# Attention over eight heads per operation, a feed-forward over 512-token blocks with another smelu, and interleaved issue

## The chip, the cores and the metric

One Trainium2 chip, one of its cores. A core has five engines with queues of their own: PE (TensorE, matmuls), DVE (VectorE), ACT (ScalarE), POOL (GpSimd) and SP (which here only issues DMAs). The metric is device time in microseconds (us) of one execution. A *ratio* is the mean time of one kernel's fast runs over the mean of the other's in the same rounds on the same chip, so it is not quite the ratio of the medians that are quoted.

## The reference, cut to what matters

```python
batch, n_heads, seq, head_dim = (4, 8, 768, 48)
for t in range(S):                                    # linear attention with a decaying state
    cur = np.einsum('bhd,bhe->bhde', u[None] * kt, vt)
    y[:, :, t] = np.einsum('bhd,bhde->bhe', rt, state + cur)
    state = w[None, :, :, None] * state + np.einsum('bhd,bhe->bhde', kt, vt)
# y becomes x: 3072 tokens x 384
h = x @ w_in                                          # 384 -> 2048
g = np.where(h >= 1, h, np.where(h <= -1, 0.0, (h + 1) ** 2 / 4))   # smelu
return g @ w_out                                      # 2048 -> 384
```

Both kernels do the attention in chunks of 128 tokens: products of R and K with powers of w, a transposition of both, a masked 128 x 128 matrix AT of their products, AT times V plus the state's share, and a step of the state. The u term is a separate number per token and head, `diag`.

## The kernel before

It goes batch by batch, chunk by chunk and head by head. A feed-forward block of 256 tokens follows each pair of chunks. Cuts are marked with `...`.

```python
for b in range(B):
    ...
    for c in range(NCH):
        for h in range(H):
            ...                                                   # three loads of 24 KB
            nc.gpsimd.tensor_copy(V, Vf)
            nc.vector.tensor_mul(RWp, R, Wpow[h])                 # all 128 x 48
            nc.vector.tensor_mul(KWi, K, Winv[h])
            nc.gpsimd.tensor_mul(KWr, K, Wrev[h])
            nc.gpsimd.tensor_mul(RK, K, u_bc[h])
            nc.vector.tensor_tensor_reduce(scr, R, RK, 1.0, 0.0, ALU.mult, ALU.add, accum_out=diag)
            ...                                                   # 2 transposes, 2 ACT copies of 48 x 128
            nc.tensor.matmul(AT_p, KWiT, RWpT, start=True, stop=True)
            nc.vector.tensor_mul(AT, AT_p, umask)
            ...                                                   # y, state step, output: 3 matmuls, 3 small operations
        if (midx + 1) * 128 % MT == 0:                            # MT = 256
            do_moe_chunk((midx * 128) // MT)

# in do_moe_chunk, for each of the 16 blocks of d_ff:
hT_p = ps.tile([128, MT], F32, name="hT_p", tag="c")              # 2 PSUM buffers, shared with y_p
... # 3 matmuls into hT_p
nc.vector.tensor_scalar(tmp, hT_p, -1.0, 1.0, ALU.max, ALU.min)
nc.scalar.activation(tmp, tmp, AF.Square, bias=half_col, scale=0.5)
nc.scalar.activation(tmp2, hT_p, AF.Relu, bias=neg1_col, scale=1.0)
nc.gpsimd.tensor_add(gT, tmp, tmp2)
... # 2 matmuls of the second layer, which need gT at once
```

## Time and profile before

| | before |
|---|---|
| time, median of 5 | 503.6 us (500.5 to 504.6) |
| span of the profiled run | 501.4 us |
| PE, DVE, ACT, POOL busy | 76, 68, 60, 65% |
| granted PE clock, mean | 0.79 |
| instructions | 10,027 |

The head of the page gives busy us, share of the span and number of instructions by engine; the clock row has the granted PE clock in tenths, in 40 slices of the span:

```profile
...
PE 379.6 (76%) x2184; PEld 180.3 (36%) x2184; DVE 341.4 (68%) x1576; ACT 302.5 (60%) x928; POOL 324.4 (65%) x993
...
PEclk9999999956956967958958859859658659669579
...
```

The groups, costliest first. A line names the source line, engine, operation, output and inputs, shape, count; then busy us in all and mean ns of one; then the engine's idle time just before, with what ended most of it:

```profile
...
L137 PE MATMUL op<-w_out_sb,gT 128*128 128x384 bf16 x384 | 107.1, 365 | 29.4 <-POOL gT L135 25.6
...
L133 ACT ACTIVATE tmp<-tmp,half_col 128x256 f32<-128x256 f32 x192 | 97.4, 507 | 35.5 <-DVE tmp L132 30.3
L132 DVE TENSOR_SCALAR tmp<-hT_p 128x256 f32<-128x256 f32 x192 | 79.7, 420 | 43.0 <-PE hT_p L125 34.3
L180 ACT COPY RWpT<-T_p 48x128 bf16<-48x128 bf16 x192 | 49.6, 258 | 75.3 <-PE T_p L178 68.9
...
L169 POOL TENSOR_TENSOR KWr<-K,Wr 128x48 bf16<-128x48 f32 x192 | 58.5, 305 | 3.3 <-DMA K<-in_k_dram 3.2
...
```

No engine is full. Every operation of the attention is there 192 times, at 209 to 305 ns for 48 or 128 columns. The table of waits (engine, line and tile that waited, what ended it, us in all, times, longest) begins with the handover of the smelu:

```profile
...
PEld L137 <- POOL gT L135: 70.3, 152, 1.1
...
```

The windows view gives busy us of PE, weight load, DVE, ACT and POOL in a stretch, then the granted clock, the DMA share and GB/s. In the middle of the run no engine is above 86%, and PE has three quarters of its clock:

```profile
...
200.00:300.00 100.00, 85.34 (x505) 41.05 (x505) 78.59 (x370) 60.95 (x200) 69.83 (x227) 0.75 0.22 45
...
```

### The profile page before, as it was taken

How to read it: one execution, taken by the hardware profiler on the slowest of the kernel's cores; microseconds unless marked ns; L12 is line 12 of the kernel's file. 1: busy time of each engine (PE TensorE's matmuls, PEld its weight loads, DVE VectorE, ACT ScalarE, POOL GpSimd, SP SyncE). 2: the span in 40 equal slices, each digit the busy share in tenths (PEclk: the TensorE clock that was granted, in tenths of full speed). 3: DMA queues.
4: the chain of work that ended last, by engine and by line, in shares of the span. 5: the costliest groups of instructions: out<-in, count | busy, mean ns of one | idle time of the engine just before them, and what ended most of it. 6: DMA issues, size and time to landing. Idle time of an engine off the chain costs nothing. (4 is left out here: it accounts for less than half of the span.)

```text
span 501.4 us, 10027 instructions
## 1 busy us (share of the span) xinstructions
PE 379.6 (76%) x2184; PEld 180.3 (36%) x2184; DVE 341.4 (68%) x1576; ACT 302.5 (60%) x928; POOL 324.4 (65%) x993
## 2 busy tenths in 40 slices
PE   0004668978778889888879888888799798798874
PEld 0002234433343343344434433434434443443431
DVE  1243666876776877878778778768768768778632
ACT  3996226736736747737747547567457457467465
POOL 5652446846756856857847848758748757768344
PEclk9999999956956967958958859859658659669579
DMA  8942211032032023032122122121231221221100
GB/s 230 238 101 37 40 33 30 25 63 42 10 71 49 13 69 52 10 76 49 39 50 44 43 52 38 48 51 30 57 52 21 54 49 26 54 52 25 38 1 32
DMA packets 89693, 26.24 MB, mean 52 GB/s; under 512 B 83872, under 2 KB 89248, under 8 KB 89248
## 3 DMA queue, kind: packets, MB, share of 16 engines
q1 hardware_dynamic: 88864, 25.20, 22.4%
q0 software_dynamic: 768, 0.40, 1.7%
q14 instruction: 44, 0.36, 0.2%
q8 instruction: 17, 0.28, 0.2%
HBM read 20.84 MB, written 4.72 MB: 51 GB/s over the span
## 5 line engine op out<-in xcount | busy, mean ns | idle before, releaser
L137 PE MATMUL op<-w_out_sb,gT 128*128 128x384 bf16 x384 | 107.1, 365 | 29.4 <-POOL gT L135 25.6
L125 PE MATMUL hT_p<-xTt,w_in_sb 128*128 128x256 bf16 x576 | 116.0, 316 | 5.2 <-ACT tmp_10630 L134 1.3
L133 ACT ACTIVATE tmp<-tmp,half_col 128x256 f32<-128x256 f32 x192 | 97.4, 507 | 35.5 <-DVE tmp L132 30.3
L132 DVE TENSOR_SCALAR tmp<-hT_p 128x256 f32<-128x256 f32 x192 | 79.7, 420 | 43.0 <-PE hT_p L125 34.3
L180 ACT COPY RWpT<-T_p 48x128 bf16<-48x128 bf16 x192 | 49.6, 258 | 75.3 <-PE T_p L178 68.9
L192 POOL CAST state_bf<-state 48x48 bf16<-48x48 f32 x192 | 40.9, 218 | 82.2 <-PE y_p L196 41.8
L178 PE MATMUL T_p<-ident,RWp 128*48 128x128 bf16 x192 | 51.3, 267 | 45.0 <-DVE RWp L165 36.0
L206 DVE SCALAR_TENSOR_TENSOR x_sb<-V,diag,y_p 128x48 bf16<-128x48 bf16 x192 | 50.2, 263 | 45.5 <-PE y_p L196 30.6
L189 DVE TENSOR_TENSOR AT<-AT_p,umask 128x128 bf16<-128x128 f32 x192 | 55.1, 287 | 31.4 <-PE AT_p L187 29.8
L125 PEld LDWEIGHTS <-w_in_sb 128*128 128x128 bf16 x576 | 51.8, 107 | 33.6 <-issue 13.9
L169 POOL TENSOR_TENSOR KWr<-K,Wr 128x48 bf16<-128x48 f32 x192 | 58.5, 305 | 3.3 <-DMA K<-in_k_dram 3.2
L167 DVE TENSOR_TENSOR KWi<-K,Wi 128x48 bf16<-128x48 f32 x192 | 58.6, 305 | 0.0
L175 DVE CUSTOM_DVE_ANT_0 scr<-R,RK 128x48 f32<-128x48 f32 x192 | 54.4, 283 | 6.2 <-POOL RK L172 6.0
L165 DVE TENSOR_TENSOR RWp<-R,Wp 128x48 bf16<-128x48 f32 x192 | 57.1, 297 | 0.1
L187 PE MATMUL AT_p<-RWpT,KWiT 48*128 48x128 bf16 x192 | 49.2, 256 | 8.8 <-ACT KWiT L184 8.1
L172 POOL TENSOR_TENSOR RK<-K,ub 128x48 f32<-128x48 f32 x192 | 54.5, 284 | 0.0
L195 PE MATMUL y_p<-V,AT 128*128 128x48 bf16 x192 | 40.7, 212 | 17.5 <-DVE AT L189 15.5
L137 PEld LDWEIGHTS <-gT 128*128 128x128 bf16 x384 | 26.0, 103 | 74.0 <-POOL gT L135 70.3
L200 DVE SCALAR_TENSOR_TENSOR state<-state,wc,st_p 48x48 f32<-48x48 f32 x192 | 47.6, 248 | 0.6
L162 POOL CAST V<-Vf 128x48 bf16<-128x48 f32 x192 | 43.3, 227 | 0.8 <-issue 0.2
L199 PE MATMUL st_p<-V,KWr 128*48 128x48 bf16 x192 | 42.3, 220 | 0.1
L178 PEld LDWEIGHTS <-RWp 128*48 128x48 bf16 x192 | 21.7, 113 | 51.7 <-DVE RWp L165 38.2
(808 smaller groups left out, 600.4 us busy)
## 6 DMA issues: line engine op xcount, KB each, us to landing
R<-in_r_dram SPq DMA_DIRECT2D x192, 24.0 KB, 1.8
K<-in_k_dram SPq DMA_DIRECT2D x192, 24.0 KB, 1.8
Vf<-in_v_dram SPq DMA_DIRECT2D x192, 24.0 KB, 1.8
out_dram<-o_sb SPq DMA_DIRECT2D x24, 192.0 KB, 2.0
w_in_f<-in_moe_w_in_dram SPq DMA_DIRECT2D x1, 3072.0 KB, 15.6
w_out_f<-in_moe_w_out_dram SPq DMA_DIRECT2D x1, 3072.0 KB, 30.2
w_bc<-in_w_dram POOLq DMA_DIRECT2D x8, 24.0 KB, 8.5
ub<-in_u_dram POOLq DMA_DIRECT2D x8, 24.0 KB, 8.7
```

Of the source, the lines that this page charges most:

```text
L125: nc.tensor.matmul(hT_p, w_in_sb[:, kk, n * 128 : (n + 1) * 128], xTt[:, kk, :], start=(kk == 0), stop=(kk == nKb - 1),)
L132: nc.vector.tensor_scalar(tmp, hT_p, -1.0, 1.0, ALU.max, ALU.min)
L133: nc.scalar.activation(tmp, tmp, AF.Square, bias=half_col, scale=0.5)
L137: nc.tensor.matmul(out_psl[j], gT[:, j * 128 : (j + 1) * 128], w_out_sb[:, n, :], start=(n == 0), stop=(n == nN - 1),)
L165: nc.vector.tensor_mul(RWp, R, Wpow[h])
L167: nc.vector.tensor_mul(KWi, K, Winv[h])
L169: nc.gpsimd.tensor_mul(KWr, K, Wrev[h])
L172: nc.gpsimd.tensor_mul(RK, K, u_bc[h])
L175: nc.vector.tensor_tensor_reduce(scr, R, RK, 1.0, 0.0, ALU.mult, ALU.add, accum_out=diag)
L178: nc.tensor.transpose(T_p[:D, :], RWp, ident)
L189: nc.vector.tensor_mul(AT, AT_p, umask)
L206: nc.vector.scalar_tensor_tensor(out=y_dst, in0=V, scalar=diag, in1=y_p, op0=ALU.mult, op1=ALU.add,)
```

## The change

Its intent: fewer and larger operations, less on the slow paths, and PE always with something to do. It has five parts. (1) Blocks hold one chunk of all four batches, so 512 tokens are one feed-forward tile. (2) Attention operations take all eight heads at once; heads are paired in 128 partitions, 64 for each, so that the two heads' matmuls lie in different rows of the array. (3) smelu is `max(h, square(clip))`, with the clip in a saturating activation. (4) Python generators interleave attention of chunk m+1, first layer of m and second layer of m-1. (5) Setup and loads are fewer and larger. Buffers change with it: three PSUM banks for the first layer, two for the second, three for attention. The diff's core:

```diff
-    ps = ctx.enter_context(tc.tile_pool(name="ps", bufs=2, space=bass.MemoryType.PSUM))
-    ops = ctx.enter_context(tc.tile_pool(name="ops", bufs=1, space=bass.MemoryType.PSUM))
+    ps_h = ctx.enter_context(tc.tile_pool(name="ps_h", bufs=3, space=bass.MemoryType.PSUM))
+    ps_o = ctx.enter_context(tc.tile_pool(name="ps_o", bufs=2, space=bass.MemoryType.PSUM))
+    ps_a = ctx.enter_context(tc.tile_pool(name="ps_a", bufs=3, space=bass.MemoryType.PSUM))
...                                   # attention of one unit: one batch, one chunk, eight heads
+        nc.gpsimd.tensor_mul(Kw[:, :, 0:D], K, Winv)          # K, R, V are 128 x 8 x 48
+        nc.gpsimd.tensor_mul(Rw[:, :, 0:D], R, Wpow)
+        nc.scalar.copy(V, Vf)
+        nc.gpsimd.tensor_mul(KU, K, u3)
+        nc.gpsimd.tensor_mul(KU, KU, R)
+        nc.vector.reduce_sum(diag, KU, axis=mybir.AxisListType.X)
+        yield
...                                   # 8 transposes
+        nc.scalar.copy(RK, tr)                                # 128 x 1024
+        yield
+        for p in range(NP):
+            for s in range(2):
+                rows = slice(s * DP, s * DP + D)
+                mm(AT_p[s][:, p, :], KT[rows, p, :], RT[rows, p, :], start=True, stop=True)
...
+            nc.vector.tensor_mul(a, AT_p[s], umask4)          # twice, 128 x 512
+        yield
...                                   # state and y matmuls, state step
+        nc.gpsimd.tensor_mul(VD, V, diag[:, :, None].to_broadcast([128, H, D]))
+        nc.vector.tensor_add(x.rearrange("q (h d) -> q h d", h=H), VD, y)
...                                   # first layer
-            nc.vector.tensor_scalar(tmp, hT_p, -1.0, 1.0, ALU.max, ALU.min)
-            nc.scalar.activation(tmp, tmp, AF.Square, bias=half_col, scale=0.5)
-            nc.scalar.activation(tmp2, hT_p, AF.Relu, bias=neg1_col, scale=1.0)
-            nc.gpsimd.tensor_add(gT, tmp, tmp2)
+        nc.scalar.activation(cl, h_p, IDENTITY_SAT240, scale=240.0)
+        nc.scalar.activation(sq, cl, AF.Square, bias=0.5, scale=0.5 / 240.0)
+        nc.vector.tensor_max(gT[m][:, n, :], sq, h_p)         # h_p is read last here
...
+    run_all(attention_steps(0))
+    for m in range(NCH + 1):
+        att = attention_steps(m + 1) if m + 1 < NCH else iter(())
+        for n in range(nN):
+            if m < NCH:
+                layer1(m, n)
+            if m > 0:
+                layer2(m - 1, n)
+            want = (n + 1) * 5 * B // nN
+            drain(att, want - done)
```

## The prediction

> **What bounds the kernel now.** No engine is saturated: the page's busy shares are PE 76%, DVE 68%, POOL 65%, ACT 60%. It is bound by many small operations handed round five engines. PE busy is mostly latency: the matmuls stream 411,000 columns, 171 us at full clock, a third of the 501 us span. The groups show 192 attention operations of each kind (24 blocks x 8 heads), each mostly fixed cost: POOL products of 48 columns 284–305 ns, ACT copies 258 ns, DVE 248–305 ns. The feed-forward runs 192 tiles of 256: DVE clip 420, ACT Square 507, ACT Relu 460, POOL add about 730 ns. The waits say the same: the weight load of the second layer waits 70 us for the POOL add. The windows table gives a granted clock of 0.71–0.76 from 100 to 480 us. The start costs 35 us (PE's first matmul): 16 activation-table loads of 1.28 us, DMA issues of w and u interleaved with them, and whole-weight loads ahead of the first inputs.
>
> **What the change does, costed.** DVE clip and Relu disappear; saturating activation and Square (ACT) plus max (DVE) replace them, 96 tiles of 512. From the copies (258 ns at 128 columns, 482 at 384: about 146+0.875/column) cl is 0.6 us and Square about 0.7. DVE from PSUM, 287 ns at 128 and 420 at 256, gives 0.69 us at 512. POOL, 305 ns at 48 and 730 at 256, is 2.04 ns/column, so 0.99 us at 384. The Trainium skill ("GPSIMD Engine Reference", section 3.1) gives 2.6 cycles per element for two inputs, 2.2 ns: agrees. So fixed costs fall eightfold on POOL but the column cost stays.
>
> Estimates per stage of 512 tokens (4 attention units, 16 tiles):
> - ACT: 16 x 1.3 + 4 x 2.05 + 4 x 0.48 = 31 us, 27–28 with the overlap of neighbours seen in the timeline.
> - PE: 49,000 feed-forward columns = 20.6 us warm; 140 small attention matmuls at about 80 ns = 11 us; 32 us.
> - POOL: 4 x (5 x 0.99 + 3 x 0.6) = 27 us.
> - DVE: 16 x 0.69 + 4 x 3.2 = 24 us.
>
> All engines are near balance, PE and ACT first. Fewer instructions: PE 1,480 matmuls from 2,184; POOL about 200 from 993.
>
> **Critical path.** Start: the fourth unit's K, R, V queue behind half a dozen loads, about 6 MB at the 230 GB/s of the early slices, 26–28 us; its chain of about 9 us follows, so the first layer starts near 38 us; only 3 table loads. Then 28 us (first stage, no second layer), four full stages at 35–38 us (PE's 32 plus waits of in-order queues), 24 us without attention, 10 us of second layer alone, 4 us tail: about 250–265.
>
> **Predicted: 258 us, range 230 to 300.** Faster 0.98, same 0.01, slower 0.01.
>
> **What would show it.** Page: PE about 70–75% busy or more with 1,480 matmuls; ACT 65–75%; POOL 60–65% at about 1.0 us per product of 384. Windows: first layer starting at 35–42 us; stages of 33–39 us; granted clock at 0.85 or more, since the array is fed more densely. The skill ("TensorE: Matmul & The Clock Gate", Part 1) says sustained activity releases the clock; before averages 0.79. Waits: no long wait on the smelu chain; attention handoffs (transposes waiting for POOL, AT for ACT's 1,024-column copy) remain.
>
> **What would make it wrong.** A clock that stays at 0.75 makes PE 42 us per stage (about 300). POOL slower on strided or broadcast operands (above 1.3 us) would make it the bound, about 36 us per stage. Three shared attention PSUM buffers and in-order queues could serialise units to over 10 us each. Downward: small matmuls nearer 55 ns and little coupling give 230.

## More of the kernel before

A scheduler in the kernel framework sets the final order of each engine's queue.

## The result, and the profile after

| | before | after |
|---|---|---|
| time, median of 5 | 503.6 us | 242.1 us (240.1 to 242.4) |
| ratio | | 0.480 (95%: 0.478 to 0.482) |
| span of the profiled run | 501.4 us | 238.4 us |
| PE, DVE, ACT, POOL busy | 76, 68, 60, 65% | 77, 58, 69, 62% |
| granted PE clock, mean | 0.79 | 0.97 |
| instructions | 10,027 | 4,187 |

The head of the page after, with the busy tenths of PE and POOL and the clock in 40 slices of 6 us each:

```profile
...
PE 182.6 (77%) x1480; PEld 100.0 (42%) x1480; DVE 137.2 (58%) x245; ACT 164.3 (69%) x296; POOL 148.6 (62%) x197
...
PE   0033543796398296789797999899999999999994
...
POOL 5297857979899998889999897955653000000000
PEclk9999999999859769999999999999999999999999
...
```

PE's share is the same as before, but in half the time. What to see is the shape: POOL at eight or nine tenths from the tenth slice to the 26th but for one, then falling to nothing, and PE full only towards the end. The groups that answer to those of before:

```profile
...
L255 DVE TENSOR_TENSOR gT<-sq,h_p 128x512 bf16<-128x512 f32 x96 | 64.0, 682 | 27.1 <-ACT sq L254 26.7
L254 ACT ACTIVATE sq<-cl 128x512 f32<-128x512 f32 x96 | 59.6, 635 | 1.6
L253 ACT ACTIVATE cl<-h_p 128x512 f32<-128x512 f32 x96 | 56.2, 597 | 13.3 <-PE h_p L250 12.8
...
L165 POOL TENSOR_TENSOR KU<-K,u_bc 128x384 f32<-128x384 f32 x24 | 24.0, 1001 | 2.2 <-DMA K<-in_k_dram 2.2
L226 POOL TENSOR_TENSOR VD<-V,diag 128x384 f32<-128x384 bf16 x24 | 19.9, 830 | 8.4 <-ACT V L163 6.6 <-DVE diag L168 1.5
...
```

Eight heads in one POOL product cost 1.00 us, where eight products of one head took 8 x 0.30 = 2.4 us. The windows by stretch say which engine sets the pace:

```profile
...
43.00:75.00 32.00, 24.58 (x183) 12.79 (x183) 17.82 (x33) 24.11 (x43) 29.52 (x34) 0.89 0.56 111
75.00:106.00 31.00, 21.13 (x173) 11.44 (x171) 17.21 (x34) 19.18 (x37) 28.27 (x37) 0.89 0.29 64
106.00:137.00 31.00, 27.71 (x252) 15.22 (x250) 23.12 (x44) 26.38 (x50) 29.30 (x38) 1.00 0.69 143
137.00:168.00 31.00, 29.72 (x272) 16.10 (x271) 23.66 (x45) 28.46 (x52) 23.31 (x31) 1.00 0.30 70
168.00:200.00 32.00, 31.64 (x276) 17.54 (x276) 21.00 (x36) 29.51 (x54) 9.00 (x12) 1.00 0.09 32
200.00:238.00 38.00, 34.78 (x210) 18.52 (x208) 14.13 (x22) 24.61 (x47) 0.00 (x0) 0.99 0.13 47
...
```

From 43 to 137 us POOL (the fifth busy figure) is at 87.1 of 94 us; from 168 us PE is at 31.6 of 32. That is work and not latency: the matmuls that start from 168 to 200 us stream 71,500 columns, an estimated 30.2 us at 216 ns for 512. ACT, at 29.5 us, is close behind. Three of the longest waits:

```profile
...
DVE diag L168 <- POOL KU L166: 40.1, 11, 12.6
DVE gT L255 <- ACT sq L254: 26.7, 29, 5.0
...
PEld L172 <- POOL KWi_158 L160: 13.0, 2, 11.6
...
```

The first is the one that matters. DVE executes its queue strictly in order. In that queue stands the sum `diag` of a later unit, ahead of the mask of the present one. It waits for POOL's product, and the mask waits with it. The timeline of DVE (start us, us, engine, line, operation; in brackets the idle time before it):

```profile
...
75.89 0.54 DVE L168 TENSOR_REDUCE diag<-KU 128x8 f32<-128x384 f32 x1
80.67 0.55 DVE L168 TENSOR_REDUCE diag<-KU 128x8 f32<-128x384 f32 x1 [4.24 <-POOL KU L166]
81.14 0.68 DVE L187 TENSOR_TENSOR AT_846<-AT_p_836,umask 128x512 bf16<-128x512 f32 x1
...
```

And PE's, in the same stretch. The matrix product that the mask was to work on (`AT_p_836`) was done at 76.5 us:

```profile
...
76.30 0.22 PE L183 MATMUL AT_p_836<-RK 48*128 48x128 bf16 x1
...
81.88 0.48 PE L201 MATMUL y<-Tbd_182,RK 128*128 128x96 bf16 x4 [4.59 <-DVE AT_846 L187]
...
```

So PE stood idle for 4.6 us behind a mask that stood behind a sum that stood behind POOL. (By the source, the matmul that waited, L201, does not read the mask's result; its output needs one of the three attention PSUM buffers, and the mask had to free it. The next matmul, L207, reads the mask's result itself.) The Trainium skill ("PSUM — Partial Sum Buffer", section "Engine vs sequencer instructions") says that the queues of ACT, DVE and POOL are strictly first in, first out, and that matmuls start in program order; the trace agrees, with these 4.2 us of DVE and 4.6 us of PE.

### The profile page after: what moved, and what is told of

It reads as the page before. It is cut to its first block, busy times and chain, and to the rows that moved or that the text cites. A ratio compares the mean times of both kernels' runs of the same rounds, so it can differ in the third digit from the quotient of the medians.

```text
span 238.4 us, 4187 instructions
## 1 busy us (share of the span) xinstructions
PE 182.6 (77%) x1480; PEld 100.0 (42%) x1480; DVE 137.2 (58%) x245; ACT 164.3 (69%) x296; POOL 148.6 (62%) x197
## 4 chain that ended last, share of the span: by engine, by line
PE 40%; POOL 22%; DVE 18%; issue 10%; ACT 7%; DMA 2%; SPq 0%; POOLq 0%; ACTq 0%; DVEq 0%
PE h_p L250 16%; PE o_p L270 16%; POOL KU L166 5%; POOL KU L165 4%; DVE gT L255 4%; POOL VD L226 3%; ACT sq L254 2%; ACT RK L176 2%; POOL KWi_158 L160 2%; POOL RWp_156 L161 2%; DVE x L228 2%; DMA K<-in_k_dram 2%; DVE diag L168 2%; ACT cl L253 2%; PE xp L232 2%
## 5 line engine op out<-in xcount | busy, mean ns | idle before, releaser
L250 PE MATMUL h_p<-xT,w_in_sb 128*128 128x512 bf16 x288 | 78.8, 391 | 9.7 <-DVE gT L255 9.1
L270 PE MATMUL o_p<-w_out_sb,gT 128*128 128x384 bf16 x384 | 80.8, 331 | 0.4 <-ACT o_sb L273 0.2
L255 DVE TENSOR_TENSOR gT<-sq,h_p 128x512 bf16<-128x512 f32 x96 | 64.0, 682 | 27.1 <-ACT sq L254 26.7
L253 ACT ACTIVATE cl<-h_p 128x512 f32<-128x512 f32 x96 | 56.2, 597 | 13.3 <-PE h_p L250 12.8
L254 ACT ACTIVATE sq<-cl 128x512 f32<-128x512 f32 x96 | 59.6, 635 | 1.6
L168 DVE TENSOR_REDUCE diag<-KU 128x8 f32<-128x384 f32 x24 | 13.2, 551 | 50.8 <-POOL KU L166 40.1
L250 PEld LDWEIGHTS <-w_in_sb 128*128 128x128 bf16 x288 | 27.3, 100 | 34.4 <-issue 15.1
L176 ACT COPY RK<-tr 128x1024 bf16<-128x1024 bf16 x24 | 24.3, 1013 | 7.2 <-PE tr L174 7.2
L165 POOL TENSOR_TENSOR KU<-K,u_bc 128x384 f32<-128x384 f32 x24 | 24.0, 1001 | 2.2 <-DMA K<-in_k_dram 2.2
L226 POOL TENSOR_TENSOR VD<-V,diag 128x384 f32<-128x384 bf16 x24 | 19.9, 830 | 8.4 <-ACT V L163 6.6
L166 POOL TENSOR_TENSOR KU<-KU,R 128x384 f32<-128x384 f32 x24 | 24.0, 1002 | 0.4
L172 PE MATMUL tr<-ident,KWi_158 128*128 128x128 bf16 x32 | 3.8, 253 | 12.8 <-POOL KWi_158 L160 12.8
L160 POOL TENSOR_TENSOR KWi_158<-K,Winv 128x384 bf16<-128x384 f32 x8 | 8.0, 1001 | 8.7 <-ACT Winv L123 6.5
L183 PEld LDWEIGHTS <-RK 48*128 48x128 bf16 x192 | 5.9, 100 | 16.5 <-ACT RK L176 11.7
L201 PEld LDWEIGHTS <-RK 128*128 128x128 bf16 x80 | 5.5, 100 | 13.3 <-issue 10.8
L232 PEld LDWEIGHTS <-x 128*128 128x128 bf16 x72 | 5.1, 106 | 11.7 <-DVE x L228 10.9
```

Of the source, the lines that this page charges most:

```text
L165: nc.gpsimd.tensor_mul(KU, K, u3)
L166: nc.gpsimd.tensor_mul(KU, KU, R)
L168: nc.vector.reduce_sum(diag, KU, axis=mybir.AxisListType.X)
L176: nc.scalar.copy(RK, tr)
L226: nc.gpsimd.tensor_mul(VD, V, diag[:, :, None].to_broadcast([128, H, D]))
L232: nc.tensor.transpose(xp[:, kk, :], x[:, kk * 128 : (kk + 1) * 128], ident)
```

## The experiments

The main theory, A: in the changed kernel POOL, with its queue in order and other engines' queues tied to it, sets the pace up to about 150 us, and PE after that. The rival, B: PE's columns bound the whole run and POOL is slack. Two further questions: what each part of the change is worth, and why.

| run | what it is | median us | against |
|---|---|---|---|
| e1 | after, old smelu | 307.1 | after +65 |
| e2 | after, POOL's products per head | 339.3 | after +97 |
| e4 | after, no interleaving in the source | 294.4 | after +52 |
| e9 | after, first layer in tiles of 256 | 258.1 | after +16 |
| e10 | after, two PSUM buffers for h_p | 265.3 | after +23 |
| e8 | after, loads of four units first | 241.0 | after -1 |
| e6 | after, one POOL product to DVE | 229.4 | after -13 |
| e7 | after, two POOL products to DVE | 227.1 | after -15 |
| e11 | after, no wait of `diag` for POOL (wrong result) | 233.5 | after -9 |
| e12 | e7 and e8 together, casts to ACT | 225.2 | after -17 |
| e3 | before, new smelu | 540.3 (one fast run) | before +37 |
| e5 | e3, h released early (wrong result) | 447.1 | before -56 |

The parts of +65, +97 and +52 must not be added: each makes POOL or the queues the bound in its own way, and the whole gain is 261 us. No run undoes the wider operations of DVE, ACT and PE in the attention, the pairing of heads, or the shorter setup; what these give is open.

### e1: the old smelu in the changed kernel

```diff
-        nc.scalar.activation(cl, h_p, IDENTITY_SAT240, scale=240.0)
-        nc.scalar.activation(sq, cl, AF.Square, bias=0.5, scale=0.5 / 240.0)
-        nc.vector.tensor_max(gT[m][:, n, :], sq, h_p)
+        nc.vector.tensor_scalar(tmp, h_p, -1.0, 1.0, ALU.max, ALU.min)
+        nc.scalar.activation(tmp, tmp, AF.Square, bias=0.5, scale=0.5)
+        nc.scalar.activation(tmp2, h_p, AF.Relu, bias=neg1_col, scale=1.0)
+        nc.gpsimd.tensor_add(gT[m][:, n, :], tmp, tmp2)
```

> The changed kernel with the old smelu back (DVE clip, Square and Relu on ACT, add on POOL), in tiles of 512; all else as it is. ACT and DVE keep their number of passes (2 and 1), PE is untouched. POOL gets 96 adds of 512 columns, about 1.25 us each by the 2.04 ns per column of before: +120 us, so about 269 us busy instead of 149. Theory A (in the changed kernel POOL paces the first two thirds, and PE only the last third): POOL becomes the bound of the whole run, 295 to 330 us. Rival B (PE's columns bound it, POOL is slack): 240 to 255 us.

307.1 us (ratio to before 0.610). The head of its page and its POOL row:

```profile
...
PE 202.3 (66%) x1459; PEld 109.3 (36%) x1480; DVE 139.7 (46%) x246; ACT 168.5 (55%) x295; POOL 265.7 (87%) x293
...
POOL 4389589999999999999999999999998998749940
...
```

POOL is busy 265.7 us, close to the 269 computed, and nearly full from end to end; ACT and DVE barely changed. A holds; B, which has POOL slack, falls. What the new smelu buys *in this kernel* is that POOL no longer has 120 us of adds.

### e2: POOL's products cut up by head

```diff
-        nc.gpsimd.tensor_mul(Kw[:, :, 0:D], K, Winv)
-        nc.gpsimd.tensor_mul(Rw[:, :, 0:D], R, Wpow)
+        for h in range(H):
+            nc.gpsimd.tensor_mul(Kw[:, h, 0:D], K[:, h, :], Winv[:, h, :])
+            nc.gpsimd.tensor_mul(Rw[:, h, 0:D], R[:, h, :], Wpow[:, h, :])
...                                   # the other three likewise
```

> The changed kernel with POOL's five products of 8 heads x 48 columns each cut into eight products of 48 columns, as before had them; every other engine keeps its work. At about 0.29 us each (before: 0.284 to 0.305) a unit's products take 11.6 us instead of 4.8, POOL about 149+163 = 312 us. Theory A: 325 to 365 us, POOL over 85% busy: the fixed cost of one engine alone gives back a third or more of the gain. Rival B: under 265 us.

339.3 us (ratio 0.674), inside A's range:

```profile
...
PE 201.3 (60%) x1458; PEld 107.8 (32%) x1480; DVE 136.9 (41%) x245; ACT 165.7 (49%) x296; POOL 266.9 (79%) x1037
...
POOL 4798998999999999999999999898999896000000
...
```

POOL's 267 us are fewer than the 312 expected, since products that follow each other overlap (48.6 us for 192 of them, 253 ns each, though one takes 286 ns). Its 79% of the span also misses "over 85%"; it is near full until about 275 us and idle while PE works off the rest. On one engine alone, the number of operations is worth 97 us.

### e3: the new smelu alone, in the kernel before

```diff
-            nc.vector.tensor_scalar(tmp, hT_p, -1.0, 1.0, ALU.max, ALU.min)
-            nc.scalar.activation(tmp, tmp, AF.Square, bias=half_col, scale=0.5)
-            nc.scalar.activation(tmp2, hT_p, AF.Relu, bias=neg1_col, scale=1.0)
-            nc.gpsimd.tensor_add(gT, tmp, tmp2)
+            nc.scalar.activation(tmp, hT_p, IDENTITY_SAT240, scale=240.0)
+            nc.scalar.activation(tmp2, tmp, AF.Square, bias=0.5, scale=0.5 / 240.0)
+            nc.vector.tensor_max(gT, tmp2, hT_p)
```

> The kernel before with only the new smelu (two ACT passes with the saturating activation, then max on DVE), tiles still 256, attention per head. POOL loses 192 adds of 0.73 us, 140 of its 324 us; DVE's 420 ns clip becomes a 420 ns max; ACT's bias operands go. Theory A (before is bound by the number of small operations handed round, of which this removes one in four of the smelu's): 430 to 475 us. Rival (the smelu is the main part of the gain): under 380 us.

A miss, and in the wrong direction: 540.3 us in its one fast run. Its other three took 549 to 559 us at a lower clock and were counted as slow, so there is no verdict; the 540.3 is 7% above the 503.1 us of before in the same rounds. POOL fell from 324 to 194 us busy, and the kernel got slower. Its longest wait is new, and its timeline shows the cause:

```profile
...
ACT tmp L133 <- PE hT_p L126: 132.0, 113, 2.3
...
```

```profile
...
314.39 0.38 ACT L133 ACTIVATE tmp<-hT_p 128x256 f32<-128x256 f32 x1 [1.77 <-PE hT_p L126]
...
315.03 0.38 ACT L133 ACTIVATE tmp<-hT_p 128x256 f32<-128x256 f32 x1 [0.26 <-PE hT_p L126]
...
315.75 0.75 DVE L135 TENSOR_TENSOR gT<-tmp,hT_p 128x256 bf16<-128x256 f32 x2
...
317.88 1.27 PE L126 MATMUL hT_p<-xTt,w_in_sb 128*128 128x256 bf16 x5
...
318.55 0.38 ACT L133 ACTIVATE tmp<-hT_p 128x256 f32<-128x256 f32 x1 [1.77 <-PE hT_p L126]
...
```

A pair of tiles passes every 4.16 us (314.39 to 318.55). The two clips follow the matmuls, then both squares, then both maxima, and only then come the next matmuls. The clip of the old smelu and its Relu were done with `hT_p` while the POOL add was still to come. The new smelu reads `hT_p` in its last step, so each of two PSUM buffers is held through the whole chain. Whether that is the cause or only the longer chain on ACT, e5 was to tell.

### e5: the same, with the PSUM tile released early (wrong result)

```diff
-            nc.vector.tensor_max(gT, tmp2, hT_p)
+            nc.vector.tensor_max(gT, tmp2, tmp)
```

> The kernel of e3 (before with the new smelu, 552 us), but the DVE max reads the two SBUF tiles instead of one SBUF tile and the PSUM tile hT_p; wrong result on purpose. Same instructions, sizes and engines; hT_p now comes free after the first ACT pass, not after the last of the three. Theory E (e3 lost because the new smelu holds each of two PSUM buffers through its whole chain, so the first layer runs two tiles, then waits: a pair of tiles every 4.18 us in e3): 440 to 490 us, so below before. Rival (two passes on ACT in series make the chain longer, wherever it reads): 530 us or more.

(The 552 us in this text is the median of all four runs of e3; its fast run is the 540.3 us.) 447.1 us (ratio 0.887). The same line of waits now reads:

```profile
...
ACT tmp L133 <- PE hT_p L126: 13.9, 44, 1.0
...
```

132 us of ACT's waiting became 14. Same instructions on the same engines; the last reader of the PSUM tile moved to the start of the chain, and DVE reads SBUF in its place (which made its maximum no cheaper: 417 ns in e3, 434 ns here). So the new smelu would be worth 56 us to the kernel before with its PSUM tile free early, and costs 37 us as it stands. (The scheduler also changed the order that it made, pairs in e3 and single tiles in e5; the two cannot be told apart, since the order follows from the buffers.)

### e10: two PSUM buffers for h_p in the changed kernel

```diff
-    ps_h = ctx.enter_context(tc.tile_pool(name="ps_h", bufs=3, space=bass.MemoryType.PSUM))
+    ps_h = ctx.enter_context(tc.tile_pool(name="ps_h", bufs=2, space=bass.MemoryType.PSUM))
```

> The changed kernel with two PSUM buffers for h_p instead of three; one bank stays unused. The new smelu holds h_p for cl, sq and max, 0.60+0.63+0.68 us plus handoffs, about 2.2, and its own three matmuls take 0.65: two buffers allow a tile per about 1.4 us, PE needs one per 1.7 us with the other work. Theory E (what made e3 slow is holding too few buffers; 512-token tiles with a second layer between hide most of it): 244 to 262 us. Rival (two buffers are enough here): 240 to 243 us.

265.3 us (ratio 0.525), 3 us above the top of the range; the direction is right and the size was estimated too small. ACT's wait for the first layer's matmuls, 12.8 us in the changed kernel, is:

```profile
...
ACT cl L253 <- PE h_p L250: 41.0, 40, 5.2
...
PE h_p L250 <- DVE gT L255: 19.7, 14, 4.5
...
```

The third bank is worth 23 us. It belongs to the new smelu as much as the formula does.

### e4: no interleaving in the source

```diff
-    run_all(attention_steps(0))
-    for m in range(NCH + 1):
...
+    for m in range(NCH):
+        run_all(attention_steps(m))
+        for n in range(nN):
+            layer1(m, n)
+        for n in range(nN):
+            layer2(m, n)
```

> The changed kernel without the generators' interleaving: the source has all attention of a chunk, then its 16 first-layer tiles, then its second layer. The order in the built program still shows attention products between feed-forward matmuls, so the framework's scheduler interleaves by itself. Theory A: within 5% of the changed kernel, 232 to 255 us. Rival D (the hand-made interleaving is what fills PE): 270 us or more.

294.4 us (ratio 0.585): rival D's prediction holds. The order of the built program did show attention among feed-forward matmuls, and I read from that that the scheduler does it by itself. It does so in part only. The last line of the view of one tile gives the busy tenths of its instructions in 40 slices; first the changed kernel's first-layer matmuls, then those of e4:

```profile
...
busy tenths in 40 slices 0000000893363065566086752976539675798500
```

```profile
...
busy tenths in 40 slices 0000009862000996000994003992005891029840
```

In e4 the first layer comes in six bursts. Between them attention runs alone, as a chain of handoffs; PE's granted clock is 0.75 and 0.74 in the stretches 200 to 225 and 250 to 270 us, and 0.87 in the mean, against 0.97. So interleaving by hand is worth 52 us.

### e9: the first layer in tiles of 256

```diff
-        for kk in range(nKb):
-            mm(h_p, w_in_sb[:, kk, n * 128 : (n + 1) * 128], xT[m][:, kk, :], start=(kk == 0), stop=(kk == nKb - 1))
+        for c0 in (0, 256):
+            for kk in range(nKb):
+                mm(h_p[:, c0 : c0 + 256], w_in_sb[:, kk, n * 128 : (n + 1) * 128], xT[m][:, kk, c0 : c0 + 256], start=(kk == 0), stop=(kk == nKb - 1))
...                                   # cl, sq and max likewise, by halves of the same tiles
```

> The changed kernel with each first-layer tile of 512 tokens done as two halves of 256 in the same PSUM bank and SBUF tiles: 96 more of each of the two ACT passes and of the DVE max, 288 more matmuls, same columns. From 0.60 and 0.635 us at 512 and 0.38 and 0.36 at 256, ACT grows by about 25 us at most, DVE by 14. Theory A says the last third is PE's, with ACT at 29 of 32 us close behind: ACT becomes the bound there, 250 to 268 us. Rival (tile size does not matter, since PE streams the same columns): 240 to 245 us.

258.1 us (ratio 0.512), in A's range. In its late stretch:

```profile
...
200.00:231.00 31.00, 30.51 (x292) 21.45 (x290) 19.80 (x47) 29.72 (x87) 0.83 (x1) 1.00 0.09 33
...
```

ACT is at 29.7 of 31 us there, but PE is at 30.5 and weight loads at 21.5, since 288 more matmuls bring 288 more loads. That ACT became the bound, as expected, is therefore not shown; both are full. (More than the tile's size changed: a half needs the attention of two batches and not of four, and the first layer starts at 29.0 us, not 43.1.)

### e6 and e7: POOL's products on DVE

```diff
-        nc.gpsimd.tensor_mul(Rw[:, :, 0:D], R, Wpow)      # e6
+        nc.vector.tensor_mul(Rw[:, :, 0:D], R, Wpow)
```
```diff
-        nc.gpsimd.tensor_mul(KU, K, u3)                   # e7, with Rw left on POOL
-        nc.gpsimd.tensor_mul(KU, KU, R)
+        nc.vector.tensor_mul(KU, K, u3)
+        nc.vector.tensor_mul(KU, KU, R)
```

> The changed kernel with one of POOL's five products (R times Wpow) on DVE: POOL 149-24 = 125 us busy, DVE 137+13 = 150. Nothing else moves by hand. Theory A (POOL paces the stretch up to about 150 us): 222 to 234 us, at most 25 us gained, since PE has 170 us of work after the first layer starts. Rival B (PE bound, POOL slack): 239 to 246 us.

> The changed kernel with both products that lead to diag (K times u, times R) on DVE: POOL 149-48 = 101 us, DVE 137+27 = 164; DVE's sum no longer waits for POOL (40 us of DVE waits, one of which held PE for 4.6 us). Theory A: 216 to 230 us, more than e6 gains, unless DVE's 1.1 us more per unit takes some back. Rival B: 239 to 250 us.

229.4 us (0.456) and 227.1 us (0.451): both in A's ranges, below B's. But moving twice the work gained only 2 us more, and e7's windows show why:

```profile
...
75.00:106.00 31.00, 28.41 (x254) 15.30 (x258) 30.75 (x54) 26.88 (x51) 20.24 (x26) 1.00 0.68 144
106.00:137.00 31.00, 27.23 (x241) 14.83 (x245) 30.50 (x53) 25.86 (x49) 20.55 (x26) 1.00 0.49 108
...
```

DVE (the third figure) has 30.8 and 30.5 of 31 us: it took POOL's place as the pace. Part of that is the price of the product on DVE. It took from 0.54 us up to 1.35, 0.84 and 0.90 in the mean for the two lines, and POOL's `VD` went from 830 to 928 ns. The Trainium skill ("GPSIMD Engine Reference", section 1, "Specifications") says that POOL's SBUF interfaces are shared with DVE and contend when DVE has two SBUF inputs. These numbers agree with that; no run isolates it.

### e11: the wait without the work (wrong result)

```diff
-        nc.vector.reduce_sum(diag, KU, axis=mybir.AxisListType.X)
+        nc.vector.reduce_sum(diag, K, axis=mybir.AxisListType.X)
```

> The changed kernel with the DVE sum reading K (loaded long before) and not KU, the last of POOL's products; wrong result on purpose. POOL still computes KU: same work on every engine, but no DVE wait for POOL's product (40 us of DVE's waits). Theory A1 (POOL's run-ahead products hold DVE's in-order queue, and through the mask the PE): 228 to 237 us. Rival A2 (POOL's amount of work alone sets the pace, as in e6): 239 to 243 us.

233.5 us (ratio 0.464), in A1's range. POOL still does all its products, 148.3 us of them:

```profile
...
PE 181.5 (78%) x1458; PEld 99.2 (43%) x1480; DVE 136.7 (59%) x245; ACT 163.9 (71%) x296; POOL 148.3 (64%) x197
...
```

```profile
...
DVE diag L168 <- POOL VD L226: 28.0, 9, 9.4
...
```

So 9 of the 13 us that e6 gained can be had without taking any work off POOL: what hurt was not only how much POOL had to do, but that another engine's queue stood still for it. About 4 of the 9 us come at the start, since the first layer begins at 39.1 us and not at 43.1. The scheduler also gave the queues another order, and what that did is not separated. (Not all of DVE's waiting went: it waits 28.0 us for POOL's `VD`, which reads an earlier `diag`, against 10.7 in the changed kernel.) In e6 the same wait fell from 40.1 to 11.6 us, so its gain holds both effects; how much of each is left open.

### e8: the first four units' loads ahead of the weights

```diff
-    load(0)
+    for i in range(4):
+        load(i)
...                                   # load(1) and the two loads among the weights go
```

> The changed kernel with the loads of the first four attention units ahead of all weights. The first layer started at 43 us, since the fourth unit's inputs came behind the first-layer weights. Theory A: first layer at 31 to 36 us and 230 to 237 us in all, about as much gained as the start is shorter. Rival (PE's column count and POOL's queue take the earlier start back, because later stages are bound by other work): 239 to 243 us.

241.0 us (ratio 0.479): nothing gained, the rival's range. Not for the rival's reason, though: the first layer started at 43.6 us, no earlier than the 43.1 of the changed kernel. DVE's timeline in e8 shows what holds the start:

```profile
...
15.17 0.55 DVE L165 TENSOR_REDUCE diag<-KU 128x8 f32<-128x384 f32 x1 [12.43 <-POOL KU L163]
19.76 0.55 DVE L165 TENSOR_REDUCE diag<-KU 128x8 f32<-128x384 f32 x1 [4.04 <-POOL KU L163]
20.23 1.28 DVE L184 TENSOR_TENSOR AT<-AT_p,umask 128x512 bf16<-128x512 f32 x2
...
30.91 3.41 DVE L242 CAST w_in_sb<-w_in_f 128x1536 bf16<-128x1536 f32 x2
34.23 1.28 DVE L184 TENSOR_TENSOR AT<-AT_p,umask 128x512 bf16<-128x512 f32 x2
...
```

The mask of the first unit (20.23) could have begun at about 14.7 us, when its matmuls ended; the sum of the second unit stood before it and waited 4.0 us for POOL. Later, two casts of weights (3.4 us) stand between two masks. The inputs were there; the queue was not free.

### e12: a version meant to beat both

e7 and e8 together, and the casts of the first-layer weights on ACT:

```diff
-            nc.vector.tensor_copy(w_in_sb[:, :, q * W : (q + 1) * W], w_in_f[q])
+            nc.scalar.copy(w_in_sb[:, :, q * W : (q + 1) * W], w_in_f[q])
```

> A version meant to beat both: the changed kernel with e7's move (both products that lead to diag on DVE), e8's load order, and the four casts of the first-layer weights on ACT, which is 1.7 us each less for DVE and took 6.8 us between the masks at the start. In e7 DVE became the pace from 43 to 137 us (92 of 94 us busy), and e8 alone gained nothing, since POOL and the DVE's queue held the four first units. Theory A: with both of those lightened the earlier loads count: first layer at 28 to 34 us instead of 38 (e7), and 217 to 224 us. Rival (PE's 170 us after the first layer, plus waits, give it back as in e8): 225 to 228 us.

225.2 us, correct, ratio to before 0.447 (0.445 to 0.449), 7% below the changed kernel. It lies in the rival's range, not in A's: the first layer starts at 36.2 us, where 28 to 34 were expected, and against e7 (ratio 0.451, another chip) little is gained. PE is now busy 182 of 225 us, and DVE is still full from 43 to 137 us (92.7 of 94).

## Why the prediction was right or wrong, point by point

- **The total: right, in part by luck.** 258 us with 230 to 300 was predicted, and 242.1 measured. But errors of opposite sign met in it. The start and the first stage took 86.5 us in the profiled run where 38 + 28 = 66 were predicted; the four full stages took 118.6 us where four times 35 to 38, 140 to 152, were predicted; the rest took 33 where 38 were.
- **Costs of single operations: right.** A POOL product of 384 columns 0.99 us predicted, 1.00 measured; cl 0.6 and 0.597; Square 0.7 and 0.635; max 0.69 and 0.682. The Trainium skill's 2.6 cycles per element for two inputs on POOL ("GPSIMD Engine Reference", section 3.1) are an estimated 2.2 ns per element at the page's 1.2 GHz; the trace's 286 ns at 48 columns (e2) and 1,001 at 384 make 2.13 ns, and so agree.
- **PE's small matmuls: too dear.** The step "140 small attention matmuls at about 80 ns = 11 us" is the term that was mis-sized, by some 5 us per stage. In the late stretch 48-column matmuls start 27 ns apart (seven starts from 146.15 to 146.31 us), transposes 56 ns apart, and paired heads start together:

```profile
...
150.92 0.23 PE L183 MATMUL AT_p_1991<-RK 48*128 48x128 bf16 x1
150.92 0.23 PE L183 MATMUL AT_p_1992<-RK 48*128 48x128 bf16 x1
150.98 0.22 PE L183 MATMUL AT_p_1991<-RK 48*128 48x128 bf16 x1
...
```

  The pairs follow each other at about 57 ns, 29 for one matmul. The Trainium skill ("TensorE: Matmul & The Clock Gate", Part 3) says that matmuls in different row groups run concurrently; the trace agrees. By these spacings a unit's attention needs about 1.5 us of PE, 6 per stage, an estimate from the trace.
- **"PE and ACT first": right for the last third, wrong before.** POOL sets the pace from 43 to 137 us (87 of 94 us), and e1, e2 and e6 show it. The prediction made POOL the bound only if a product cost more than 1.3 us; at 1.0 us it was one all the same. The reasoning took sums per stage and left out what e11 measures: a busy in-order queue stops the queues that wait for it. Stages were then unequal, not 35 to 38 us each: the first-layer matmuls of blocks 0 to 5 (48 each, 288 records in all) begin at 43.1, 86.5, 119.9, 148.9, 178.0 and 205.1 us. So the first stage took 43 us, where 28 were predicted for a stage without a second layer (the scheduler moved 36 of block 0's 64 second-layer matmuls into it), and the four full ones took 33, 29, 29 and 27.
- **The start: wrong in its cause.** "The fourth unit's K, R, V queue behind half a dozen loads" gave 38 us; it was 43.1, outside the stated 35 to 42. e8 put the loads first and the start stayed at 43.6 us. The chain of in-order queues on POOL and DVE is what runs over the start: e11, with the loads where they were and DVE's wait for `KU` gone, brought 39.1, and e12, which lightened the chain further, 36.2.
- **The clock: right.** 0.95 to 0.97 in the five runs, where 0.85 or more was predicted, and the two dips of the clock row follow slices in which PE's row is at 3 and at 2 tenths. The Trainium skill ("TensorE: Matmul & The Clock Gate", Part 1) says that the clock is throttled by default and that sustained activity releases it, which agrees. How much of the gain is the clock's own, no run isolates, and it stays open.
- **Waits: half right.** The wait of AT for ACT's copy (11.7 us) was there as said; of the transposes' wait for POOL (12.8 us), 11.6 are one wait at the very start. The longest, DVE's sum for POOL's product (40.1 us, of which 12.6 are one wait at the start), was not foreseen, and on the smelu chain, where no long wait was expected, DVE waited 26.7 us for ACT's square, 5.0 at the longest.
- **Parts that were not priced.** Interleaving by hand (e4: 52 us) and the third PSUM bank (e10: 23 us) have no number in the prediction. They were within the result only because the stage estimate assumed that engines overlap.

## What to carry to other kernels

Count operations before columns: eight heads in one product took 1.0 us where eight products took 2.4, and going back to eight on POOL alone cost 97 us here. When a rewrite moves the *last reader* of a PSUM tile to the end of a chain, give the tile another buffer in the same step, or the better formula loses (540 against 447 us). With in-order queues, ask of every instruction not only whether its engine has time but what stands behind it: a sum placed early, with a mask behind it, waited for POOL, and taking that wait away gained 9 us (e11).

## What the Trainium skill lacked or had wrong

- "TensorE: Matmul & The Clock Gate", section "Back-to-back issue gap": for a sustained stream of weight load and matmul pairs it gives about 131 ns per matmul at N=512 and about 81 ns at N=128. Here, in such streams at clock 1.00, matmuls of 512 columns start 215 to 216 ns apart, and transposes of 128 columns 56 ns apart. For 512 it is too low, for 128 too high; the gap that the same section gives for an isolated warm matmul, N/2.4 + 2.5 ns (216 and 56), fits both.
- "ScalarE: Activation LUTs", section "Table sets": it says that Ln then Exp need one table load, since one set has both. The kernel before shows 16 loads of 1,283 ns, one for each change between Ln and Exp; whether one load serves both must be looked up in the trace.
- "GPSIMD Engine Reference", section 3.1: it gives one rate for two inputs. The product `VD` took 830 ns at 384 columns, the products of two full f32 inputs 1,001 ns. `VD` differs in two things, a bf16 input and an f32 input that repeats one number over 48 columns. `X` times `wc`, both f32 and one repeated in the same way, took 507 ns at 192 columns, where a line through 286 ns at 48 and 1,001 at 384 gives an estimated 592. So the type alone does not explain it; no run separates the two.
- "PSUM — Partial Sum Buffer": neither it nor another page ties the number of buffers for a PSUM tile to when its last reader comes. Here the same operations took 540 us (one fast run) with the last reader at the end of the chain and 447 us with it at the start (e3, e5).
